# A mixed attention and expert kernel: the second and third expert computed in two row tiles of 64

## The chip, the cores and the metric

The kernel runs on one core of a Trainium2 chip. The engines of a core have a queue each and work side by side: TensorE (matmuls; in the profile PE, its weight loads PEld), VectorE (DVE), ScalarE (ACT), GpSimd (POOL) and SyncE (SP), which here issues DMAs and passes on semaphores. The metric is the device time of one execution in microseconds (us), less being better. Times are the median of several executions; the profile is of one further execution.

## What is computed

The output is `g * a + (1 - g) * b` for 2048 tokens of width 448. `a` is a linear attention with a learned softmax feature map (16 heads of 28), `b` a mixture of 8 experts of which each token uses the best two, `g` a sigmoid gate per token.

```python
def _B_ref(x, w_gate, w1, w2):               # E = 8 experts, K = 2, F = 1792
    logits = xf @ w_gate
    topk_idx = jnp.argsort(-logits, axis=-1)[:, :K]
    topk_val = jnp.take_along_axis(logits, topk_idx, axis=-1)
    gates = _softmax(topk_val, axis=-1)
    for e in range(E):
        mask = (topk_idx == e)
        w = (gates * mask).sum(-1, keepdims=True)
        h = _silu(xf @ w1[e]) @ w2[e]         # 448 -> 1792 -> 448
        out = out + w * h
```

All of it is in float32. The kernel splits each operand of a matmul into a rounded part and a remainder (h and l below) and adds three products: high x high, high x low, low x high.

## The kernel before

**Stages.** The first part computes attention, routing and the table of which token goes to which expert. The expert part follows: one loop (L1321) over `s`, 8 experts times 14 chunks of 128 hidden rows, `e, fc = divmod(s, 14)`. Experts are taken in the order of their number of tokens; `ROOMS` gives the columns kept for each: 552, 544, 544, 504, 504, 504, 496, 488. The first three have more than 512 (`LARGE = 3`); the columns above 512 are their extra ones, `extra(e)`: 40, 32, 32. Where these are 32 the expert is called narrow, and the second layer of the extra columns is done at the end of the expert, for all chunks together, by `side_by_side` from raw weights (L1143), which are kept for it in buffers named `kept`.

**One chunk.** The first layer gives `hp` (128 hidden rows x tokens) in PSUM from the weights w1 and the gathered tokens `xgh`, `xgl`. `gated` puts it through silu on ScalarE (L1076) into `hs`, and VectorE splits that into `hx` (L1082, L1085; the extra columns go to `hxe`, L1080). The second layer multiplies `hx` with w2 and adds into `acc`, one PSUM bank for each 128 tokens (c = 0 to 3, and 4 for the extra ones). After chunk 13 `leave` scales each `acc` into `y` (L1194 on ScalarE for odd c, L1196 on VectorE for even c) and GpSimd scatters it with an indirect DMA that adds into the output (L995).

**Two forms.** Experts 0 to 2 used the full array of 128 rows. `first` (L1054) runs a chunk in two pieces of half the columns (276 or 272), 11 matmuls each (L145): the 448 input rows lie in four groups of 128, the last of them holding 64 rows twice, so that the three products take 4 + 4 + 3 matmuls. `second` and `share` (L1161) run the second layer one or two chunks behind, with the list `held`.

Experts 3 to 7 use two row tiles: the array as two halves of 64 rows that work at the same time, each on its own PSUM bank. `first_pair` (L1046) takes two chunks at once, each with a bank of its own. In `in_halves` (L1031) a round is two matmuls, one in each half. The seven groups of 64 input rows are shared out over 12 rounds and, after a change of sides, 9 turned rounds, in which each bank is written from the other half of the array (L1043). `second_pair` (L1114) does the same for the second layer of two chunks in 24 rounds (L1127). The loop draws these rounds from a generator `queue` with `go_on(n)`, 12 in each chunk: in an even chunk 12 first rounds, 12 second ones, 9 turned ones; in an odd chunk 12 second ones.

**Hand-overs.** The two halves may not write one bank at the same time, and nothing in TensorE's queue orders them. So when a bank goes from one half to the other, `meet` (L1015) puts a nop in SyncE's queue (L1020) which waits for a matmul that lies at most `APART = 24` matmuls back, and the first matmul of the other half waits for the nop. SyncE's queue keeps its order: the nops stand in line with the weight loads of `stage` (L773), and `behind_` ties both into one sequence.

**Order.** TensorE, ScalarE and VectorE have the order written out by the program in the expert part. In each step ScalarE and VectorE first split the weights of a later chunk (`halve`, L796 and L798), and from chunk 9 on transpose and split one tile of the next expert's tokens (`tokens`, L869, L849, L854); from chunk 4 on GpSimd issues two gathers of those tokens per chunk (`gathers`, L829). PSUM has two banks for `hp`, four for `acc` with c = 0, 1 and 4, and one pair for c = 2 and 3.

Of the kernel before, what the change touches and what calls it, by code (L numbers as in the profile page):

```python
# [9 lines left out]
F32R = mybir.dt.float32r  # L10
# [8 lines left out]
P = 128  # L19
# [66 lines left out]
FILL = ((0, 0), (0, 1))  # L86
APART = 24


@with_exitstack  # L90
def gated_mix(ctx: ExitStack, tc: tile.TileContext, xt, xq, wk, wq, wv, wphi, wo, w12, out):
# [765 lines left out]
    def tokens(e, c):  # L857
        if c == 0:
            pool = pf if e % 2 else pw
            xg[e] = (pool.tile([P, 4, CAP], F32R, tag="xgh", name=f"xgh{e}", bufs=1),  # L860
                     pool.tile([P, 4, MAIN] if e >= LARGE else [P, 3, CAP], F32R, tag="xgl", name=f"xgl{e}", bufs=1))
        xgh, xgl = xg[e]
        if (e, c) not in xg:
            return
        t = xg[e, c]
        n, m = (4, P) if c < nm else (-(-extra(e) // 32), extra(e))
        xt_ = pm.tile([P, 4, P], F32, tag="xt", name=f"xgt{e}{c}")
        for b in range(n):
            nc.vector.transpose(xt_[:, :, b * 32:(b + 1) * 32], t[:, b].rearrange("p (c k) -> p c k", c=4))  # L869
        yield  # L870
        m = min(m, ROOMS[e] - c * P)
        at = slice(c * P, c * P + m)
        both(xgh[:, :, at], xgl[:, :, at], xt_[:, :, 0:m], e >= LARGE)

# [155 lines left out]

    def in_halves(o, xh, xl, wh, wl):  # L1031
        rounds = []
        for own, turned_ in (((0, 1, 2, 3), False), ((0, 1, 2), True)):
            for s in own:
                for w, x in ((wh, xh), (wl, xh), (wh, xl)):
                    one = [(1 - a if turned_ else a, a) for a in range(2)]
                    rounds.append([(i, a, w[half[a], s, i * P:(i + 1) * P], x[half[a], s])
                                   for i, a in (reversed(one) if turned_ else one)])
# [7 lines left out]
    def first_pair(e, pair):  # L1046
        n = ROOMS[e]
        xgh, xgl = (x[:, :, 0:n] for x in xg[e])
        hp = [bank("A", f"hp{e}_{2 * pair + i}")[:, 0:n] for i in range(2)]
        yield from in_halves(hp, xgh, xgl, *wts[e * (NFC // 2) + pair, 1])  # L1050
        for i in range(2):
            gated(e, 2 * pair + i, 0, hp[i])

    def first(e, fc, hf):  # L1054
# [37 lines left out]
    def accs(e):  # L1092
        own = [nm, 0, 1] if extra(e) else [0, 1] if e + 1 < E else range(nm)
        a = {c: bank("O", f"acc{e}{c}") for c in own}
# [19 lines left out]
    def second_pair(e, pair):  # L1114
# [3 lines left out]
        if narrow(e) and ends:  # L1118
            for at in range(0, NFC, BATCH):
                side_by_side(e, range(at, min(at + BATCH, NFC)))  # L1120
        todo = [(c, l, r) for c in range(nm) for i in range(2) for l, r in products(e, 2 * pair + i, c)]
        n = len(todo) // 2
# [8 lines left out]
        if ends:  # L1131
            leave(e, (2, 3, *order(e)[:-2]))
            if e == E - 2:
                settle()
# [94 lines left out]
    for t in range(NT + 2):  # L1229
# [67 lines left out]
        if SPLIT <= t < SPLIT + 3 and splits:  # L1297
            if next(splits[0], 0) == 0:
                del splits[0]
                if splits:  # L1300
# [11 lines left out]
    held = []  # L1312
    queue = (h for e, pair in [(LARGE - 1, NFC // 2 - 1), *((e, pair) for e in range(LARGE, E)
                               for pair in range((NFC - LATE * (e == E - 1)) // 2))] for h in second_pair(e, pair))
# [6 lines left out]
    for s in range(E * NFC):  # L1321
        e, fc = divmod(s, NFC)
        k, i = divmod(s, 2)
        token = tokens(e + 1, fc - 9) if e + 1 < E and 9 <= fc <= 9 + nm else iter(())
        next(token, 0)
# [8 lines left out]
        if e + 1 < E and fc >= 4:  # L1334
            for _ in range(2):
                next(asked, None)
        if e < LARGE:
            for hf in range(2):
# [3 lines left out]
            advance(1)  # L1342
            while len(held) > (1 if e == 0 or fc == 0 else 2):
                h = held.pop(0)
# [6 lines left out]
        if e == E - 1 and fc > NFC - LATE:  # L1351
            n = n // 2 if fc < NFC - 1 else 0
        if fc % 2 == 0:
            f = first_pair(e, fc // 2)
# [119 lines left out]
```

## Time and profile before

| what | value |
|---|---|
| median of 3 runs | 792.58 us (791.54 to 792.87) |
| the profiled execution | 790.7 us |
| its span, first to last instruction | 789.0 us |
| mean granted clock of TensorE | 0.995 |
| HBM read, written | 72.31 MB, 12.82 MB |
| instructions | 18466 |

How to read the lines that follow below. In the groups of instructions a row is: line, engine, operation, what it writes <- what it reads, the shape (64*128 is a weight tile of 64 rows and 128 columns), xcount, then busy us and the mean ns of one, then idle us of that engine just before them with what ended it. In the timeline a row starts with the start in us and the length in us; several instructions of one kind are merged. In a row of the waits stands who waited for whom, us in total, times, the longest. Matmuls are pipelined: a matmul's length includes its way through the array, so the price of one in a stream is the distance between two starts.

### The profile page before, as it was taken

Reading aid. Unit: us, or ns where it says so; the run is one execution under the profiler, and the core shown is the slowest. Engines: PE = TensorE matmul, PEld = TensorE weight load, DVE = VectorE, ACT = ScalarE, POOL = GpSimd, SP = SyncE. Lnnn points to the kernel's source line nnn. Section 1 sums busy time; section 2 is a strip of 40 time slices with the busy share of each in tenths; the row PEclk is TensorE's granted clock in tenths of the full one; section 3 lists DMA queues with packets and bytes.
Section 4 is the critical chain, followed back from the end, with each engine's and each line's share of the span. In section 5 each row is a group of like instructions: output and inputs, shape, how many; then the busy total and the mean of one; then the engine's idle time right before and its main releaser. Section 6 shows DMA issues by size and latency. Waiting matters only on the chain. (4 is left out here: it accounts for less than half of the span.)

```text
span 789.0 us, 18466 instructions
## 1 busy us (share of the span) xinstructions
PE 776.7 (98%) x7542; PEld 721.9 (91%) x7542; DVE 481.6 (61%) x1045; ACT 308.9 (39%) x521; POOL 338.3 (43%) x320
## 2 busy tenths in 40 slices
PE   9999999999999999999999998999999999999996
PEld 7888888888999999998998897999999999999995
DVE  4798978778776865665575443544754555475442
ACT  5543455666533443343342322332432333343220
POOL 4667877875123235414540435144325405423102
PEclk9999999999999999999999998999999999999999
DMA  8420000144333336326541452363345436434502
GB/s 282 118 86 1 2 2 26 39 103 143 125 137 127 108 88 179 100 83 144 160 131 54 105 162 90 108 153 128 120 116 152 130 112 157 136 135 116 171 2 47
DMA packets 39756, 86.37 MB, mean 109 GB/s; under 512 B 11338, under 2 KB 20722, under 8 KB 39668
## 3 DMA queue, kind: packets, MB, share of 16 engines
q1 hardware_dynamic: 29332, 67.88, 26.0%
q0 software_dynamic: 10192, 17.03, 11.2%
q8 instruction: 61, 1.00, 0.6%
q10 hardware_dynamic: 144, 0.23, 0.1%
q14 instruction: 27, 0.22, 0.1%
HBM read 72.31 MB, written 12.82 MB: 108 GB/s over the span
## 5 line engine op out<-in xcount | busy, mean ns | idle before, releaser
L829 POOL DMA_INDIRECT xg<-in_xq_dram,idq x114 | 127.1, 1115 | 155.2 <-PE hp L1043 55.5
L1076 ACT ACTIVATE hs<-hp 128x272 f32<-128x272 f32 (+4 forms) x154 | 70.8, 483 | 312.2 <-issue 175.0
L1127 PE MATMUL acc<-w2h,hx 64*128 64x448 f32 (+3 forms) x1088 | 192.0, 363 | 0.1
L1082 DVE CAST hx<-hs 128x504 fp32r<-128x504 f32 (+5 forms) x154 | 55.1, 358 | 209.3 <-ACT hs L1076 196.4
L1127 PEld LDWEIGHTS acc<-w2h,hx 64*128 64x128 f32 (+3 forms) x1088 | 159.8, 182 | 5.0 <-ACT y L1194 1.5
L1127 PE MATMUL acc<-w2l,hx 64*128 64x448 f32 (+3 forms) x544 | 152.4, 364 | 0.0
L1043 PE MATMUL hp<-xgh,w1h 64*128 64x504 f32 (+2 forms) x490 | 144.8, 390 | 2.5 <-issue 2.5
L1043 PE MATMUL hp<-xgh,w1l 64*128 64x504 f32 (+2 forms) x490 | 144.7, 389 | 0.0
L1043 PE MATMUL hp<-xgl,w1h 64*128 64x504 f32 (+2 forms) x490 | 144.4, 388 | 0.0
L995 POOL DMA_INDIRECT out_dram<-y,tabm x30 | 49.3, 1643 | 158.1 <-DVE y L1196 150.8
L1161 PE MATMUL acc<-w2h,hx 128*128 128x448 f32 (+2 forms) x366 | 111.7, 365 | 0.0
L1127 PEld LDWEIGHTS acc<-w2l,hx 64*128 64x128 f32 (+3 forms) x544 | 95.8, 182 | 1.5
L1043 PEld LDWEIGHTS hp<-xgh,w1h 64*128 64x128 f32 x490 | 87.4, 186 | 6.0 <-issue 3.9
L1043 PEld LDWEIGHTS hp<-xgl,w1h 64*128 64x128 f32 x490 | 87.7, 187 | 2.2
L1043 PEld LDWEIGHTS hp<-xgh,w1l 64*128 64x128 f32 x490 | 87.4, 187 | 2.0
L1085 DVE TENSOR_TENSOR hx<-hs,hx 128x276 fp32r<-128x276 f32 (+5 forms) x168 | 84.9, 512 | 5.3
L145 PE MATMUL hp<-xgh,w1h 128*128 128x272 f32 (+1 forms) x336 | 87.9, 289 | 0.0
L145 PE MATMUL hp<-xgh,w1l 128*128 128x272 f32 (+1 forms) x336 | 87.7, 289 | 0.0
L798 DVE TENSOR_TENSOR w1l<-wr,w1h 128x1024 fp32r<-128x1024 f32 x56 | 68.3, 1219 | 11.1 <-ACT w1h L796 9.9
L1161 PEld LDWEIGHTS acc<-w2h,hx 128*128 128x128 f32 (+2 forms) x366 | 68.0, 186 | 6.2 <-issue 0.7
L1161 PE MATMUL acc<-w2l,hx 128*128 128x448 f32 (+2 forms) x190 | 69.4, 365 | 0.0
L145 PEld LDWEIGHTS hp<-xgh,w1h 128*128 128x128 f32 x336 | 63.2, 188 | 0.7
(239 smaller groups left out, 1398.4 us busy)
## 6 DMA issues: line engine op xcount, KB each, us to landing
wr<-in_w_dram SPq DMA_DIRECT2D x56, 512.0 KB
wr<-in_w_dram SPq DMA_DIRECT2D x46, 448.0 KB
kept<-in_w_dram SPq DMA_DIRECT2D x10, 448.0 KB
out_dram<-aos SPq DMA_DIRECT2D x16, 224.0 KB
xr<-in_xt_dram SPq DMA_DIRECT2D x10, 256.0 KB
xg<-in_xq_dram,idq POOLq DMA_INDIRECT x114
xr<-in_xt_dram SPq DMA_DIRECT2D x6, 192.0 KB
out_dram<-zero SPq DMA_DIRECT2D x5, 224.0 KB
```

The costliest lines, as they stand in the source:

```text
L145: reached["pe"] = nc.tensor.matmul(o, a, b, start=i == 0, stop=i == n - 1)
L798: nc.vector.tensor_tensor(out=l, in0=raws[s][layer - 1], in1=h.bitcast(F32), op=ALU.subtract)
L829: i = nc.gpsimd.indirect_dma_start(out=t[:, b], out_offset=None, in_=xq, in_offset=bass.IndirectOffsetOnAxis(ap=idq[:, e, 4 * c + b:4 * c ...
L995: return nc.gpsimd.indirect_dma_start(out=out, out_offset=bass.IndirectOffsetOnAxis(ap=idx_ap, axis=0), in_=y, in_offset=None, compute_op= ...
L1043: meet(("first", i), a, lambda: nc.tensor.matmul(o[i], l, r, start=n == 0, stop=n == len(rounds) - 1), n == 0)
L1076: nc.scalar.activation(hs[:, tsl], hp, AF.Silu)
L1082: nc.vector.tensor_copy(h[:, tsl], hs[:, tsl])
L1085: nc.vector.tensor_tensor(out=h[:, a + o:b + o], in0=hs[:, a:b], in1=h[:, a:b].bitcast(F32), op=ALU.subtract)
L1127: meet((e, c), a, lambda: nc.tensor.matmul(acc[e][c][:l.shape[1], 0:D], l[half[a]], r[half[a]], start=new, stop=ends and c not in of[k + 1 ...
L1161: i = nc.tensor.matmul(acc[e][c][:l.shape[1], 0:D], l, r, start=fc == 0 and k == 0, stop=fc == NFC - 1 and k == len(pr) - 1)
```

## The change

The experts from `TILED = 1` on, so now also 1 and 2, run in row tiles; only expert 0 keeps the full array. For experts 1 and 2, whose 544 columns do not fit in one PSUM bank, a new `first_pieces` gives the two halves of the columns (272) of one chunk to the two banks, with the same 12 and 9 rounds. Their chunk runs 12 first rounds, `LEAD = 6` second rounds, 9 turned rounds and 6 second rounds; the first two chunks of expert 1 run 7 and 7, since they finish the last pair of expert 0, which has 28 rounds. The low part `xgl` of their tokens gets a fourth group.

The banks of `acc` are asked for in another order for experts 1 and 2, their second layer takes c in the order 0, 2, 1, 3, and `LEAVING` gives the order in which the `acc` of experts 0, 1 and 2 are emptied. During expert 0, three gathers are issued per chunk instead of two, and the tokens of expert 1 are split from chunk 8 on. Expert 0 holds its last two chunks back for the queue.

```diff
+LEAVING = ((4, 2, 3, 0, 1), (0, 2, 3, 4, 1), (2, 3, 0, 4, 1))
+TILED = 1
+LEAD = 6
...
-                     pool.tile([P, 4, MAIN] if e >= LARGE else [P, 3, CAP], F32R, tag="xgl", name=f"xgl{e}", bufs=1))
+                     pool.tile([P, 4, MAIN if e >= LARGE else CAP] if e >= TILED else [P, 3, CAP], F32R, tag="xgl", name=f"xgl{e}", bufs=1))
...
-        both(xgh[:, :, at], xgl[:, :, at], xt_[:, :, 0:m], e >= LARGE)
+        both(xgh[:, :, at], xgl[:, :, at], xt_[:, :, 0:m], e >= TILED)
...
-    def in_halves(o, xh, xl, wh, wl):
+    def in_halves(o, ops):
...
-                for w, x in ((wh, xh), (wl, xh), (wh, xl)):
+                for w, x in ((2, 0), (3, 0), (2, 1)):
                     one = [(1 - a if turned_ else a, a) for a in range(2)]
-                    rounds.append([(i, a, w[half[a], s, i * P:(i + 1) * P], x[half[a], s])
+                    rounds.append([(i, a, ops[i][w][half[a], s], ops[i][x][half[a], s])
...
+    def first_pieces(e, fc):
+        s, i = divmod(e * NFC + fc, 2)
+        w = [x[:, :, i * P:(i + 1) * P] for x in wts[s, 1]]
+        n = ROOMS[e] // 2
+        hp = [bank("A", f"hp{e}_{fc}_{hf}")[:, 0:n] for hf in range(2)]
+        yield from in_halves(hp, [(*(x[:, :, hf * n:(hf + 1) * n] for x in xg[e]), *w) for hf in range(2)])
+        for hf in range(2):
+            gated(e, fc, hf, hp[hf])
...
-        own = [nm, 0, 1] if extra(e) else [0, 1] if e + 1 < E else range(nm)
+        own = [nm, 0, 1] if e < TILED else [0, 1, nm] if extra(e) else [0, 1] if e + 1 < E else range(nm)
...
-        todo = [(c, l, r) for c in range(nm) for i in range(2) for l, r in products(e, 2 * pair + i, c)]
+        todo = [(c, l, r) for c in ((0, 2, 1, 3) if narrow(e) else order(e)) for i in range(2)
+                for l, r in products(e, 2 * pair + i, c)]
...
-            leave(e, (2, 3, *order(e)[:-2]))
+            leave(e, LEAVING[e] if extra(e) else (2, 3, 0, 1))
...
-    queue = (h for e, pair in [(LARGE - 1, NFC // 2 - 1), *((e, pair) for e in range(LARGE, E)
+    queue = (h for e, pair in [(TILED - 1, NFC // 2 - 1), *((e, pair) for e in range(TILED, E)
...
-        token = tokens(e + 1, fc - 9) if e + 1 < E and 9 <= fc <= 9 + nm else iter(())
+        at = fc - (9 if e else 8)
+        token = tokens(e + 1, at) if e + 1 < E and 0 <= at <= nm else iter(())
...
-            for _ in range(2):
+            for _ in range(2 if e else 3):
                 next(asked, None)
-        if e < LARGE:
+        if e < TILED:
...
-            while len(held) > (1 if e == 0 or fc == 0 else 2):
+            while len(held) > (1 if fc < NFC - 1 else 2):
...
-        if fc % 2 == 0:
+        if extra(e):
+            a, b = (7, 7) if (e, fc) in ((1, 0), (1, 1)) else (LEAD, n - LEAD)
+            f = first_pieces(e, fc)
+            next(f)
+            go_on(a)
+            next(f, None)
+            go_on(b)
+        elif fc % 2 == 0:
```

More of the change, by code (lines that the diff above doesn't have):

```diff
@@ L1049, in first_pair @@
         hp = [bank("A", f"hp{e}_{2 * pair + i}")[:, 0:n] for i in range(2)]
-        yield from in_halves(hp, xgh, xgl, *wts[e * (NFC // 2) + pair, 1])
+        yield from in_halves(hp, [(xgh, xgl, *(w[:, :, i * P:(i + 1) * P] for w in wts[e * (NFC // 2) + pair, 1]))
+                                  for i in range(2)])
         for i in range(2):
             gated(e, 2 * pair + i, 0, hp[i])
+    def first_pieces(e, fc):
[6 more added lines that the diff above has]
+            gated(e, fc, hf, hp[hf])
     def first(e, fc, hf):
```

## The prediction

> **What bounds the kernel now.** First the page's engine shares, then the timeline of TensorE at one expert of each kind, then the waits.
>
> ```profile
> PE 776.7 (98%) x7542; PEld 721.9 (91%) x7542; DVE 481.6 (61%) x1045; ACT 308.9 (39%) x521; POOL 338.3 (43%) x320
> ```
>
> TensorE (PE) is busy for 776.7 us, 98% of the span, so a change is worth what it takes out of TensorE's own stream, less the waits that it puts in. The chain of waits starts at the very last scatter and says nothing here. The expert stage, with the window rows of one plain chunk, one tiled pair and the one hole:
>
> ```profile
> 340.53:345.72 5.19, 5.19 (x36) 5.02 (x35) 4.28 (x13) 2.38 (x4) 0.94 (x1) 1.00 0.20 36
> 454.45:464.11 9.66, 9.66 (x93) 9.66 (x91) 4.33 (x7) 2.86 (x4) 1.33 (x1) 1.00 0.64 178
> 481.00:484.00 3.00, 0.73 (x4) 0.32 (x3) 0.61 (x2) 1.27 (x3) 2.09 (x3) 0.93 0.82 291
> 484.00:493.00 9.00, 8.78 (x54) 7.97 (x56) 6.40 (x15) 2.85 (x4) 3.94 (x4) 0.64 0.12 31
> ```
>
> Columns: length, then busy time of PE, weight loads (PEld), VectorE (DVE), ScalarE (ACT), GpSimd (POOL), then granted clock, DMA share, GB/s. PE fills the first two windows, at full clock. At 481 us, inside the fourth expert (e=3), it stands for 2.3 and 0.2 us and has a clock of 0.64 for 9 us (a loss of 9 x 0.36 = 3.2): 5.7 us, in a stage whose code the change leaves alone.
>
> A chunk (128 of the 1792 hidden rows) of the second expert (e=1) in the old form, then rounds of the tiled form of e=3:
>
> ```profile
> 337.77 0.29 PE L145 MATMUL hp<-xgh,w1h 128*128 128x272 f32 x1
> ...
> 340.53 0.36 PE L1161 MATMUL acc<-w2h,hx 128*128 128x448 f32 x1
> ...
> 342.96 0.29 PE L145 MATMUL hp<-xgh,w1h 128*128 128x272 f32 x1
> ...
> 439.48 0.37 PE L1127 MATMUL acc<-w2h,hx 64*128 64x448 f32 x2
> ...
> 441.90 0.39 PE L1043 MATMUL hp<-xgh,w1h 64*128 64x504 f32 x2
> ...
> 444.42 0.39 PE L1043 MATMUL hp<-xgl,w1h 64*128 64x504 f32 x2
> ```
>
> First layer: 22 matmuls in 340.53 - 337.77 = 2.76 us, 0.1255 each. Second layer: 12 in 2.43, 0.2025 each. Tiled: 12 rounds of two 64-row matmuls in 441.90 - 439.48 = 2.42, so a round of 448 columns costs what one full matmul of 448 does; a round of 504 costs 2.52 / 11 = 0.229.
>
> **The change part by part.**
>
> *First layer of e=1 and e=2 in row tiles.* The 448 input rows are seven halves of 64, times three products: 21 rounds in place of 22 matmuls, on the same 272 columns. No row shows a tiled round of 272. At the full matmul's price, 0.1255, each chunk saves one: 28 chunks x 0.1255 = **-3.5 us**. Bounds: the line through the tiled 504 (0.229, 0.2286 by the pair: (9.66 - 24 x 0.2025) / 21) and 448 (0.2025) leads to 0.1205 at 272, which would save 21 x 0.005 x 28 = 2.9 us more; from the other side, 0.229 lies 0.002 over the line of the two full rows (0.2025 + 56 x 0.00044 = 0.227), and with more than twice that on top a round would cost 0.131 and save nothing. I take 0.1255: same columns, nearest row.
>
> *Weight loads.* A round has two loads where a full matmul has one.
>
> ```profile
> L730 PE MATMUL et<-ident,eq 64*128 64x64 f32 x224 | 10.0, 229 | 0.0
> L145 PEld LDWEIGHTS hp<-xgh,w1h 128*128 128x128 f32 x336 | 63.2, 188 | 0.7
> ```
>
> The transposes of L730 load 64x128 weights for every matmul, in row tiles: 224 in 10.0 us, 45 ns each, so two loads fit in 89 ns, under 126. Cost nothing. The Trainium skill, "TensorE: Matmul & The Clock Gate", section "LDWEIGHTS (loading the stationary operand)", prices a load by its columns alone, at 1.2 GHz: 128 columns are 107 ns, whatever the rows; two in turn would be 213 ns, a round longer than its matmul. By that rule 21 rounds would be 4.5 us; row L730 speaks against it.
>
> *Second layer.* Rounds and matmuls are equal in number and price: 0. The two readings above, 2.42 and 2.43, tell nothing below a hundredth, and a hundredth in 26 chunks is 0.3; I put in +0.2 (0 to 0.3). The last two chunks of e=0 become a queued pair of 28 rounds for 28 matmuls: 0.
>
> *e=0 into e=1.* The last first-layer piece of (0,13) used to be followed by 14 second-layer matmuls. Now the first rounds of (1,0) come straight behind it and need both hp banks at once. Rows of the release:
>
> ```profile
> 468.54 0.37 PE L1127 MATMUL acc<-w2h,hx 64*128 64x448 f32 x1
> 468.62 0.39 PE L1043 MATMUL hp<-xgl,w1h 64*128 64x504 f32 x1
> ...
> 469.09 1.07 ACT L1076 ACTIVATE hs<-hp 128x504 f32<-128x504 f32 x2 [6.83 <-PE hp L1043]
> ...
> 482.73 1.07 ACT L1076 ACTIVATE hs<-hp 128x504 f32<-128x504 f32 x2 [10.78 <-remote]
> ...
> 483.38 1.27 PE L1043 MATMUL hp<-xgh,w1h 64*128 64x504 f32 x2 [2.27 <-issue]
> ```
>
> ```profile
> L1076 ACT ACTIVATE hs<-hp 128x504 f32<-128x504 f32 x42 | 22.6, 589 | 121.3 <-issue 66.0 <-PE hp L1043 44.6 <-remote 10.8
> L1076 ACT ACTIVATE hs<-hp 128x272 f32<-128x272 f32 x56 | 22.2, 397 | 75.3 <-PE hp L145 44.6 <-issue 30.7
> ```
>
> Silu starts 469.09 - 469.01 = 0.08 after the last matmul's end; PE starts 483.38 - (482.73 + 0.59) = 0.06 after silu's. So from the start of the last matmul: 0.29 + 0.08 + 0.40 + 0.06 = 0.83, where the next would have started after 0.13: **+0.7 us**, once. The hole's 2.3 us cost 3.2 more by the lowered clock; 0.7 us is a third of it, and I let it cost 0.7. The Trainium skill, "TensorE: Matmul & The Clock Gate", section "HAM oscillation — how this bites in real kernels", puts the limit at gaps of some 3.4 us; by it neither gap would lower the clock, and the hole's 2.3 us did.
>
> *Six rounds ahead of the turned ones.* Each chunk now runs 12 first rounds, 6 second, 9 turned first, 6 second. Two things must fit in six rounds (6 x 0.2025 = 1.22 us). One: SyncE sees the last of the 12 and frees the banks for the other row tile: 0.29 + 0.08 to see it, 0.06 to start, 0.19 a load = 0.62, in 1.22 + 0.13 = 1.35: spare 0.7.
>
> ```profile
> L1020 SPq EVENT_SEMAPHORE  x132: 17/17/17, 435.4 to 769.0; - x132
> SPq L773 <- PE acc L1143: 15.9, 1, 15.9
> L1127 PE MATMUL acc<-w2h,hx 64*128 64x448 f32 x824 | 179.4, 363 | 0.1
> ```
>
> 132 hand-overs now leave PE 0.1 us idle on L1127, with 12 rounds of cover. I put in +0.2 us for all new ones (0 to 1). Queued behind a hand-over on SyncE are the weight loads of L773, and the reverse: the load of e=2's third pair waits for the raw weights that L1143 still reads (15.9 us in one wait), and the first hand-over of pair (1,6) stands behind it. L1143 is done with that buffer after its second batch of four:
>
> ```profile
> 358.60 0.96 PE L1143 MATMUL acc<-wr,hxe 128*32 128x448 f32 x8
> 359.37 2.06 PE L1143 MATMUL acc<-kept,hxe 128*32 128x448 f32 x24
> ```
>
> ```profile
> 273.29 0.33 SPq L773 DMA_DIRECT2D kept<-in_w_dram  x1
> ```
>
> That is some 0.7 us into the 2.0, and the load's issue takes 0.33: hidden, 0.5 us once if not. Two: both silus after the turned rounds must free both hp banks before the next chunk. Silus start (1.07 - 0.59) = 0.48 apart at 504, 0.48 - 0.19 = 0.29 at 272: 0.29 + 0.08 + 0.29 + 0.40 + 0.06 = 1.12 of 1.35. Spare 0.2 us, the thinnest cover of the change; cost 0, priced as a rival.
>
> *Orders at expert changes.* At (1,2) and (2,2) the second bank of the new expert is the one that the first y of the old expert leaves; VectorE comes to it after the chunk's hx work.
>
> ```profile
> L1082 DVE CAST hx<-hs 128x272 fp32r<-128x272 f32 x28 | 8.8, 313 | 31.1 <-ACT hs L1076 28.6 <-issue 2.5
> L1082 DVE CAST hx<-hs 128x240 fp32r<-128x240 f32 x28 | 8.3, 296 | 0.0
> L1085 DVE TENSOR_TENSOR hx<-hs,hx 128x272 fp32r<-128x272 f32 x28 | 12.4, 443 | 1.0
> L1085 DVE TENSOR_TENSOR hx<-hs,hx 128x240 fp32r<-128x240 f32 x28 | 11.5, 409 | 1.0
> L1080 DVE COPY hxe<-hs 128x32 f32<-128x32 f32 x28 | 5.5, 196 | 13.1 <-ACT hs L1076 12.5 <-issue 0.6
> L1196 DVE TENSOR_SCALAR y<-acc,tabm 128x448 f32<-128x448 f32 x15 | 9.8, 679 | 2.6 <-PE acc L1161 2.5
> ```
>
> From the last turned matmul: first silu 0.77, five operations 1.66, y 0.68, release 0.06: 3.17 us. PE needs the bank after 0.13 + 1.22 + 12 x 0.1255 = 2.85. Up to 0.3 late each; the rows overlap a little, so 0 to 0.3: **+0.4** for both. The other banks have six rounds more. For e >= 3 the order is unchanged.
>
> *First gather sooner.* 17 indirect DMAs are issued in six chunks of e=0 in place of nine, three per chunk; one takes GpSimd 0.94 us (the only one in the first window above), so 2.8 us of a chunk of over 5, on an engine that is busy 43%. The token work moves from chunks 9 to 13 to chunks 8 to 12, the same VectorE and ScalarE operations plus one larger subtraction for two: off the path. It answers the 14 x 0.2025 = 2.8 us that no longer lie between (0,13) and (1,0). If that cover is gone: the length of a token step's tail, about 1 us once.
>
> **Sum:** -3.5 + 0.2 + 0.7 + 0.2 + 0.4 = -2.0 us, in the profiled execution from 790.7 (span 789.0) to 788.7. The median of the runs is 792.58, 1.9 above the profiled one; I carry the difference over: **790.6 us**. A measurement of this kernel can tell about 0.2%, 1.6 us, from no change: faster is below 791.0, slower above 794.2.
>
> **The rivals.**
>
> *Silu's cover is too short (slower).* The two row tiles do not march in step: in the tiled pair one starts its second layer at 468.54 while the other's last first-layer matmul starts at 468.62, and a tile that is ahead takes from the 0.2 us spare. If the next chunk waits 0.17 us on average in 26 chunks, that is 4.4 us: 795.0. It decides from 2.0 / 26 = 0.08 us per chunk. For it: spare 0.2 only, ScalarE also serves weight splits. Against: a tile that is ahead has slack itself, and ScalarE is busy for 2.38 of 5.19 us in a chunk, with that work lying before the silus.
>
> *The change does not do what it says:* a round of 272 in tiles costs 0.131, 21 are worth 22, and only the 1.5 us of waits remain: 794.1.
>
> *Two loads bind the round.* If loads go no faster than a 504 round proves (0.229 for two), 21 rounds take 4.8 us: +2.05 x 28 = 57 us, 848. L730 all but rules it out. It is the skill's price of a load that points this way.
>
> *The hole at 481 goes* (or is smaller), because the work before it is shifted: another 5.7 us, 785. Nothing in the diff touches what it waits for (ScalarE's silu, put down to "remote"), and it can as well be in no run that is timed.
>
> **How the numbers follow.** Forecast 0.60 (0.42 faster, 0.18 same), silu's cover 0.15 (0.13 slower, 0.02 same), no shorter round 0.11 (0.06 same, 0.05 slower), loads 0.02 slower, the hole 0.12 faster. Faster 0.54, same 0.26, slower 0.20. The range goes down to the cheaper round (790.6 - 2.9 = 787.7, with 0.7 more if no wait comes) and up past the silu case: 787.0 to 795.6; the hole's case and the dear ends above are left out, 0.2 in all.
>
> **What would show it.** In the new trace: starts of L1043 of 272 columns 0.1255 apart per round (right) or 0.13 and more (wrong); a chunk of e=1 in 5.07 us in place of 5.19; idle time of PE before the first L1043 of (1,0) of 0.7 us, released by ScalarE; none before the other chunks of e=1 and e=2 (a regular 0.1 to 0.3 there is the silu rival); no PE wait ended by SyncE. A second hole with a lowered clock anywhere, or the present one missing, would make the time wrong by 3 to 6 us without touching the working above.

## The result, and the profile after

The changed kernel took **799.64 us** (median of 6 runs, 797.94 to 800.46) where the kernel before, beside it, took 792.24 (791.2 to 792.87): a ratio of 1.0102, 95% interval 1.0089 to 1.0116. Forecast were 790.6 us and a range of 787.0 to 795.6. The profiled execution took 799.95 us, with a span of 798.2. From the page of the changed kernel, the busy line, the granted clock in 40 slices, and the group of its first layer with the idle time ahead of it at the end:

```profile
PE 777.8 (97%) x8442; PEld 725.9 (91%) x8442; DVE 475.0 (60%) x1035; ACT 306.3 (38%) x521; POOL 339.4 (43%) x320
PEclk9999999999999999999989998999999999999999
L1046 PE MATMUL hp<-xgh,w1h 64*128 64x272 f32 (+3 forms) x882 | 216.1, 345 | 8.4 <-SPq L1023 4.1
```

Three windows of the same execution (length, then busy time of PE, weight loads, VectorE, ScalarE, GpSimd, then clock, DMA share, GB/s): chunks of e=2, later chunks of e=2, and e=3.

```profile
377.00:387.00 10.00, 10.00 (x136) 9.95 (x134) 5.01 (x12) 3.09 (x6) 3.13 (x3) 1.00 0.61 159
395.00:410.00 15.00, 10.52 (x100) 9.16 (x98) 2.59 (x6) 1.75 (x4) 10.32 (x10) 0.80 0.39 115
485.00:497.00 12.00, 7.73 (x47) 5.59 (x46) 3.40 (x9) 2.35 (x4) 7.59 (x8) 0.83 0.39 126
```

The first window is what was forecast: PE is full. Apart from the chunks at the two expert changes and the places named next, the chunks of e=1 and e=2, read off the starts of their first L1046, are 5.05 to 5.16 us long, against 5.19 before. The loss is local. In 15 us of e=2 PE stands for 4.5 us and then runs at a lower clock (0.50 for some 6.8 us); chunk (2,8) takes 12.5 us. The hole in e=3 is longer than before (a gap of 3.9 us in place of 2.3), and (1,5) loses 1.5 us. Against a stream of matmuls at the prediction's prices the three places cost 8.1, 2.3 more than before, and 1.5; with some 0.8 at the expert changes and -3.4 in the regular chunks that makes +9.3, and the spans differ by 9.2.

The timeline of the worst place, TensorE (PE) and GpSimd (POOL):

```profile
400.16 0.39 PE L1046 MATMUL hp<-xgl,w1h 64*128 64x272 f32 x2
400.42 1.55 POOL L832 DMA_INDIRECT xg<-in_xq_dram,idq  x1 [0.30 <-issue]
401.83 0.47 PE L1141 MATMUL acc<-w2h,hx 64*128 64x448 f32 x2 [1.28 <-SPq L1023]
...
402.92 0.41 PE L1141 MATMUL acc<-w2h,hx 64*128 64x448 f32 x2
403.52 0.94 POOL L832 DMA_INDIRECT xg<-in_xq_dram,idq  x1 [0.30 <-issue]
404.77 0.94 POOL L832 DMA_INDIRECT xg<-in_xq_dram,idq  x1 [0.30 <-issue]
405.44 0.59 PE L1046 MATMUL hp<-xgh,w1h 64*128 64x272 f32 x1 [2.11 <-SPq L1023]
406.02 0.94 POOL L832 DMA_INDIRECT xg<-in_xq_dram,idq  x1 [0.30 <-issue]
406.83 0.59 PE L1046 MATMUL hp<-xgh,w1h 64*128 64x272 f32 x1 [0.81 <-SPq L1023]
```

The last of the first rounds ends at 400.55. The turned rounds need only to know that; SyncE's nop (L1023) waits for nothing else and SyncE issues nothing else in this stretch, and yet they start at 405.44. The nop got TensorE's semaphore 4.8 us late. Meanwhile GpSimd issues gathers without a pause, ten of them from 395.15 to 408.20, one every 1.25 to 1.85 us. The semaphore events of the trace say the same by themselves: when the updates of TensorE's semaphore are set beside the modelled ends of the matmuls that raise it, they are late only where gathers stand close together and nowhere else in the expert stage: about 0.85 us behind a pair in e=1 and e=2, and up to 2.3, 6.2 and 3.5 us in the trains of four and of ten gathers that begin at 306, 395 and 477 us. Not every such place shows it (several runs of four in the later experts stay below 0.1 us), and the scatters alone show none. The waits of the changed kernel (who for whom, us in total, times, longest):

```profile
PEld hp L1046 <- SPq L1023: 5.1, 3, 2.5
PE hp L1046 <- SPq L1023: 4.1, 3, 2.1
PE hp L1046 <- ACT hs L1089: 4.1, 2, 3.9
```

The trains were in the profile of before already. There GpSimd's timeline has, up to the silu of the prediction's hole, this (the last of them spaced alike):

```profile
475.28 0.94 POOL L829 DMA_INDIRECT xg<-in_xq_dram,idq  x1 [0.30 <-issue]
476.53 0.94 POOL L829 DMA_INDIRECT xg<-in_xq_dram,idq  x1 [0.30 <-issue]
...
481.53 0.94 POOL L829 DMA_INDIRECT xg<-in_xq_dram,idq  x1 [0.30 <-issue]
```

The scatters of the extra columns (L998, up to four of them, each waiting for the one before to land) hold GpSimd's queue for 20 us and more behind an expert change; the gathers meant two to a chunk pile up behind them and then go out in a run. One thing is different there. By the same measure the semaphores of the kernel before are at most 0.01 us late behind the pairs of e=1, and 0.8 us in a run of ten gathers beside e=2 (384.7 to 398.0 us), both computed in the full-array form; the 3.2 us behind its hole belong to e=3, which is tiled.

**Theory T1**: trains of gathers make TensorE's semaphores late; the old form of e=1 and e=2 had some 3 us of cover against that, the tiled form 0.1 to 0.7. **Rivals**: T2, the covers are short in every chunk; T3, the gathers' traffic is at work, not their issue; and, from the first results on, T4, the lateness belongs to the chip.

### The profile page after: what moved, and what is told of

It is laid out like the page before. It is cut to its first block, busy times and chain, and to the rows that moved or that the text cites. A ratio compares the mean times of both kernels' runs of the same rounds, so it can differ in the third digit from the quotient of the medians.

```text
span 798.2 us, 20347 instructions
## 1 busy us (share of the span) xinstructions
PE 777.8 (97%) x8442; PEld 725.9 (91%) x8442; DVE 475.0 (60%) x1035; ACT 306.3 (38%) x521; POOL 339.4 (43%) x320
## 5 line engine op out<-in xcount | busy, mean ns | idle before, releaser
L1141 PE MATMUL acc<-w2h,hx 64*128 64x448 f32 (+4 forms) x1540 | 276.1, 364 | 1.7 <-SPq L1023 1.3
L1046 PE MATMUL hp<-xgh,w1h 64*128 64x272 f32 (+3 forms) x882 | 216.1, 345 | 8.4 <-SPq L1023 4.1
L1141 PEld LDWEIGHTS acc<-w2h,hx 64*128 64x128 f32 (+4 forms) x1540 | 215.7, 184 | 7.6 <-ACT y L1208 1.6
L1046 PE MATMUL hp<-xgh,w1l 64*128 64x272 f32 (+3 forms) x882 | 214.7, 344 | 0.0
L1046 PE MATMUL hp<-xgl,w1h 64*128 64x272 f32 (+3 forms) x882 | 214.1, 343 | 0.0
L1141 PE MATMUL acc<-w2l,hx 64*128 64x448 f32 (+4 forms) x772 | 203.2, 364 | 0.1
L1046 PEld LDWEIGHTS hp<-xgh,w1h 64*128 64x128 f32 x882 | 142.1, 187 | 14.3 <-ACT hs L1089 5.6
L1046 PEld LDWEIGHTS hp<-xgl,w1h 64*128 64x128 f32 x882 | 141.7, 187 | 1.9
L1046 PEld LDWEIGHTS hp<-xgh,w1l 64*128 64x128 f32 x882 | 141.6, 187 | 1.8
L1141 PEld LDWEIGHTS acc<-w2l,hx 64*128 64x128 f32 (+4 forms) x772 | 125.5, 184 | 1.2
L998 POOL DMA_INDIRECT out_dram<-y,tabm x30 | 49.2, 1640 | 177.5 <-DVE y L1210 170.4
L799 ACT ACTIVATE w1h<-wr 128x1024 fp32r<-128x1024 f32 x56 | 59.2, 1057 | 0.0
L1175 PE MATMUL acc<-w2h,hx 128*128 128x448 f32 (+2 forms) x140 | 42.9, 366 | 0.0
L998 POOL DMA_INDIRECT out_dram<-y,tabx x10 | 15.3, 1534 | 64.2 <-DVE y L1210 38.8
```

Source lines behind the costliest of these rows:

```text
L799: nc.scalar.activation(h, raws[s][layer - 1], AF.Copy)
L998: return nc.gpsimd.indirect_dma_start(out=out, out_offset=bass.IndirectOffsetOnAxis(ap=idx_ap, axis=0), in_=y, in_offset=None, compute_op= ...
L1046: meet(("first", i), a, lambda: nc.tensor.matmul(o[i], l, r, start=n == 0, stop=n == len(rounds) - 1), n == 0)
L1141: meet((e, c), a, lambda: nc.tensor.matmul(acc[e][c][:l.shape[1], 0:D], l[half[a]], r[half[a]], start=new, stop=ends and c not in of[k + 1 ...
L1175: i = nc.tensor.matmul(acc[e][c][:l.shape[1], 0:D], l, r, start=fc == 0 and k == 0, stop=fc == NFC - 1 and k == len(pr) - 1)
```

## The experiments

Each group ran on one chip, with the kernel before beside it. The number is the chip's; "in time" and "late" are my words for the two sorts that turned up.

| chip | before, us | kernel: median us, ratio to before with its 95% interval |
|---|---|---|
| first measurement | 792.24 | changed: 799.64, 1.0102 (1.0089 to 1.0116) |
| 14, in time | 784.0 | a_defer: 780.95, 0.9953 (0.9937 to 0.9970); b_defer: 783.85, 0.9999 (0.9989 to 1.0008); a_reuse: 781.39, 0.9959 (0.9945 to 0.9973); b_reuse: 784.05, 0.9998 (0.9989 to 1.0008) |
| 2, in time | 784.3 | changed (a_again): 780.77, 0.9957 (0.9940 to 0.9973); a_defer2: 780.76, 0.9957 (0.9943 to 0.9971) |
| 4, in time | 784.65 | a_silu: 791.75 and b_silu: 787.15 (one run each); a_lead8: 788.4, 1.0051 (1.0035 to 1.0068); a_lead2: 781.55, 0.9960 (0.9947 to 0.9972) |
| 3, in time | 784.09 | a_safe: 780.58, 0.9955 (0.9939 to 0.9972); a_late: 780.82, 0.9962 (0.9947 to 0.9976) |
| 0, late | 789.61 | a_wide: 780.72, 0.9885 (0.9849 to 0.9920) |
| 6, late | 791.38 | changed (a_third): 799.72, 1.0120 (1.0087 to 1.0152); a_defer3: 785.95, 0.9925 (0.9903 to 0.9948) |
| 11, late | 790.92 | a_spread: 786.03, 0.9946 (0.9929 to 0.9964); b_defer2: 784.67, 0.9926 (0.9909 to 0.9943) |
| 7, in time | 784.21 | a_calm: 780.19, 0.9948 (0.9932 to 0.9965) |

### The trains taken away, in both kernels

Deferred scatters (a_ from the changed kernel, b_ from the kernel before):

```diff
+                met["gather"] = i
...
+    later = []
+    def one_later():
+        e, v, ids = later.pop(0)
+        i = scatter_add(v, ids)
+        after(i, done[e - 1] if e else rows_done)
+        follow(i, met["gather"])
+        done[e].append(i)
...
+            if c == nm:
+                later.extend((e, v, ids) for v, ids in todo)
+                continue
...
+        if later and fc in (4, 6, 8, 10):
+            one_later()
```

No gathers for experts 2 to 7, which compute on the tokens of expert 1 instead (reuse):

```diff
     def gathers(e):
+        if e > 1:
+            xg.update({(e, c): xg[1, c] for c in range(nm + (extra(e) > 0))})
+            return
```

> The changed kernel, with the scatters of the extra columns not issued in one run behind the four main scatters of an expert but one each in chunks 4, 6, 8 and 10 of the next expert, behind that chunk's gathers. All work is kept. GpSimd's queue is then free when the gathers are asked for, so no train of four and more gathers stands in it. Theory T1 (while GpSimd issues gathers back to back, the others see TensorE's semaphores late, and the tiled form of e=1 and e=2 has only 1.2 us of cover for that): the idle gaps of TensorE at 310 us and 398 to 407 us and the one in e=3 vanish with their lowered clock, some 1.5 + 8.1 + 8.5 us less: 781 to 785 us, and no chunk of e=1 or e=2 but the first two is longer than 5.3 us. Theory T2 (the covers of silu and SyncE are too short in every chunk, whatever GpSimd does): no change, 798 to 801. Theory T3 (the gathers' traffic, not their issue, disturbs the others): the same bytes are moved with more spacing, so 785 to 795, the gaps smaller and spread over more chunks.

> The kernel before the change, with the same deferral of the extra columns' scatters. All work is kept. T1: the hole at 481 us of e=3 is the same thing as the gaps of the changed kernel, so it goes with its lowered clock, 5.5 us: 785.5 to 788 us. T2, by which the hole in e=3 belongs to something else: 792, unchanged. T3: 787 to 791.

> The changed kernel without the gathers of experts 2 to 7: they compute on the tokens of expert 1, so the output is not the reference's; scatters, token work and all matmuls are kept. T1 and T3: no gather after 340 us, so no gap of TensorE after that, and only the one at 310 us (the gathers of e=2 during e=1) gone too: 780 to 785 us. T2: 798 to 801.

> The kernel before the change, again without the gathers of experts 2 to 7 (tokens of expert 1 used in their place; the output is not the reference's). T1 and T3: the hole at 481 us goes, 785 to 788 us. T2: 792, unchanged. Beside a_reuse it gives the price of the change without gathers: by the prediction's sum a_reuse should be about 2 to 3.5 us below b_reuse.

The times of the two a_ kernels look like T1: 781. But b_defer and b_reuse are equal to the unaltered kernel before, which on this chip took 784.0, 8 us less than in the first measurement. There was no hole to take away. And in none of the four traces is a semaphore late behind a pair of gathers, where the first measurement had 0.85 us. The runs settle nothing on T1; T4 comes up. T2 falls: the covers are the same here, and the chunks of a_defer are 5.05 to 5.08 us long.

### The changed kernel on another chip

No edit for a_again; a_defer2 is a_defer once more.

> The changed kernel itself, unaltered. The four kernels before ran on a chip where the kernel before takes 784.0 us and not 792.2, and their traces show no late semaphore of TensorE at all, not even behind pairs of gathers that stood as close as in the first trace. So two readings are open. T1 (trains of gathers on GpSimd delay TensorE's semaphores, on any chip): the changed kernel has its gaps in every place, 10 to 18 us above the version with deferred scatters. T4 (the late semaphores belong to the chip or the moment, not to the program): where the kernel before takes about 784, the changed one takes 780 to 783, with no gap but the 0.2 us at (1,0), and where it takes 792, the changed one takes 798 to 801.

> The version with deferred scatters again, beside the unaltered one on the same chip. T1: 10 to 18 us below the unaltered changed kernel wherever it runs. T4: the same as the unaltered one within 2 us where the kernel before takes 784; where that takes 792, T4 says nothing and T1 says 781 to 785.

T4's number: 780.77, and a_defer2 the same. Here the change makes the kernel 0.43% faster. From the page of a_again:

```profile
PE 769.3 (99%) x8442; PEld 724.7 (93%) x8442; DVE 477.3 (61%) x1035; ACT 305.8 (39%) x521; POOL 338.3 (43%) x320
PEclk9999999999999999999999999999999999999998
L1046 PE MATMUL hp<-xgh,w1h 64*128 64x272 f32 (+3 forms) x882 | 219.9, 340 | 0.2 <-ACT hs L1089 0.2
```

and the windows of the same stages:

```profile
375.00:385.00 10.00, 10.00 (x134) 9.83 (x132) 4.93 (x12) 3.07 (x7) 2.75 (x2) 1.00 0.61 161
395.00:410.00 15.00, 15.00 (x200) 14.99 (x198) 10.35 (x29) 5.87 (x12) 12.21 (x10) 1.00 0.45 151
485.00:497.00 12.00, 12.00 (x116) 11.94 (x114) 8.55 (x18) 5.71 (x10) 6.17 (x6) 1.00 0.36 121
```

From 395 to 410 us GpSimd issues ten gathers here too, a little further apart (busy 12.21 us), and pairs of them elsewhere as close as in the first measurement; PE is full, at full clock, and of 8.4 us idle ahead of L1046 0.2 are left. So a train of gathers alone does not make a semaphore late: it does so on some chips, or at some moments.

### How much cover each form has

To price a late hand-over on a chip that is in time, I made the lateness myself: extra silus, and other values of LEAD.

```diff
+        for _ in range({(1, 4): 3, (1, 8): 6, (2, 8): 12}.get((e, fc), 0) if hf == 0 else 0):
+            nc.scalar.activation(hs[:, tsl], hp, AF.Silu)
         nc.scalar.activation(hs[:, tsl], hp, AF.Silu)
```

```diff
-LEAD = 6
+LEAD = 8
```

> The changed kernel with the first silu of three chunks done several times over: 3 extra ones of 272 columns at (1,4), 6 at (1,8), 12 at (2,8). From the prediction's working two silus of this size start 0.29 us apart, so both silus of these chunks come some 0.9, 1.7 and 3.5 us late. It stands for a late semaphore of one known length, on whatever chip. The prediction gave the silus 0.2 us to spare in the tiled form of e=1 and e=2. If that is the cover, TensorE stands 0.7, 1.5 and 3.3 us behind those chunks, and the last one lowers the clock as the hole of 2.3 us did: 5.5 us of stalls and some 3 us of slow clock, 785 to 791 us where the unaltered changed kernel takes 780.8. If the cover is larger (a theory by which the late semaphores of the first measurement needed no thin cover, only their length), the first two leave no gap.

> The kernel before with the same extra silus in the same three chunks. In its form the next use of a bank comes some 3.8 us after its last matmul (11 matmuls of the other piece and 12 of the second layer), so 3.3 us are to spare: no gap from the first two, 0 to 0.5 us from the third, 784 to 785 us. If the plain form were as sensitive as the tiled one, 789 to 793.

> LEAD = 8: eight second rounds before the turned ones and four after, in every chunk of e=1 and e=2 but the first two. The silus' cover falls by 2 x 0.2025 = 0.41 us, from 0.2 to spare to 0.2 short. If the prediction's working of that cover holds, TensorE waits 0.2 us in each of 26 chunks: 5 us more than the unaltered changed kernel, 786 (784 to 787). If the two tiles that are out of step absorb it, or the silus are earlier than worked out: 781.

> LEAD = 2: two second rounds between the first and the turned rounds, so SyncE's hand-over has 0.13 + 0.41 = 0.54 us in place of 1.35 and needs 0.62 by the prediction's working: 0.1 us short in 26 chunks, 2 us more than the unaltered changed kernel, 783 (782 to 784.5). If SyncE is as quick as TensorE's own turn, 781; if a hand-over is dearer than worked out (the nop stands behind weight loads, or takes 0.3 us more), 788 or more.

An extra silu cost 0.43 us, not 0.29 (12 of them took 5.1 us), so the delays are 1.3, 2.6 and 5.1 us. In a_silu the first two delays cost 1.2 and 2.5 us, over their chunk and the next one together: **the cover is 0.1 us**. The third lengthens its own chunk by 4.8 us and costs 2.7 us more in the next one, at the lowered clock (7.75 us in place of 5.06). Windows around the three in a_silu:

```profile
305.00:311.00 6.00, 5.39 (x67) 4.92 (x65) 2.44 (x6) 2.55 (x7) 3.89 (x4) 1.00 0.41 93
322.00:334.00 12.00, 10.09 (x130) 9.62 (x128) 5.95 (x16) 5.65 (x13) 4.06 (x4) 1.00 0.30 93
398.00:416.00 18.00, 13.54 (x140) 13.15 (x138) 7.15 (x19) 9.04 (x21) 9.79 (x10) 0.81 0.42 136
```

The gaps of 0.6 and 1.9 us leave the clock at 1.00; that of 4.5 lowers it, as in the first measurement. In b_silu one wait is left of all three:

```profile
PE hp L145 <- ACT hs L1078: 1.9, 1, 1.9
```

5.1 us late, 1.9 us of stall: the old form had some 3.2 us of cover, where 3.3 was worked out. a_lead8 is 7.6 us above a_again, 0.29 per chunk: taking 0.41 away from the silus leaves them 0.29 short, so 0.12 was to spare. No wait of PE shows this, since the matmuls of the waiting half are recorded as longer; it is read off the chunks, 5.34 us in place of 5.06. a_lead2 is 0.8 us above a_again, 0.03 per chunk: SyncE's hand-over needs little more than the 0.54 us that it had. These runs were on another chip than a_again; before differs by 0.35 us between the two.

### The sooner gather undone, and more cover

```diff
-        at = fc - (9 if e else 8)
+        at = fc - 9
...
-            for _ in range(2 if e else 3):
+            for _ in range(2):
```

That is a_late; a_safe is a_defer with `LEAD = 4`.

> The changed kernel without the sooner first gather: two gathers per chunk during e=0 and the tokens of e=1 split from chunk 9 on, as before the change. The prediction put this edit at 0 and, with its cover gone, at about 1 us once: 780.8 to 782 where the kernel before takes 784, with a gap of TensorE ahead of (1,0) if the tokens are late.

> Deferred scatters and LEAD = 4: the silus' cover grows by 0.41 us, from 0.1 to 0.5 to spare, and SyncE's shrinks as much, which the run with LEAD = 2 priced at nothing or nearly. If the kernel before takes about 784 here (semaphores in time): as the unaltered changed kernel, 780 to 782, since its chunks of 5.06 us are full already. If it takes about 792 (semaphores late behind gathers): by T1 780 to 785, because there are no trains any more and lone pairs of gathers come 0.85 us late at most; by the theory that on such a chip any gather disturbs, 788 to 796.

Both as on a chip that is in time: 780.82 and 780.58. The sooner gather is worth nothing there, as the prediction had it; a_late has no gap ahead of (1,0) but the 0.17 us of a_again.

### A chip with late semaphores again: issue or traffic

In a_wide one gather of 2 KB rows fetches a tile's tokens in place of four of 512-byte rows; inside a tile the tokens come in another order.

```diff
+            if c < nm and e > 1:
+                i = nc.gpsimd.indirect_dma_start(
+                    out=t.rearrange("p a k -> p (a k)"), out_offset=None, in_=x_rows,
+                    in_offset=bass.IndirectOffsetOnAxis(ap=idm[:, e * nm + c:e * nm + c + 1], axis=0))
+                after(i, [reached["pe"]])
+                for _ in range(4):
+                    yield
+                continue
```

> The changed kernel with one gather of 128 rows of 2 KB in place of four of 512 B for each 128 tokens of experts 2 to 7 (the tokens come in another order inside a tile, so the output is not the reference's): the same bytes, a quarter of GpSimd's issues, no trains. Where the kernel before takes 784 here: 780 to 782, nothing to win. Where it takes 792: T1 (GpSimd's issuing in trains delays the semaphores) 780 to 785; T3 (the traffic of the gathers delays them) 792 to 801, with gaps of TensorE while the gathers run.

On chip 0 the kernel before took 789.61 us. With a quarter of the issues and the same bytes the changed kernel took 780.72, and PE is full through the stage that had the long gaps:

```profile
375.00:410.00 35.00, 35.00 (x462) 34.95 (x460) 20.01 (x52) 12.03 (x24) 9.61 (x8) 1.00 0.50 149
```

The latest semaphore of the expert stage is 0.53 us late, behind a pair of these gathers. GpSimd's DMA queue moved the same bytes, first in a_third (a run of the unaltered changed kernel that follows below), then in a_wide (packets, MB, share of 16 engines):

```profile
q0 software_dynamic: 10192, 17.03, 11.2%
q0 software_dynamic: 9040, 17.03, 11.0%
```

Against T3, for T1. The 1152 packets fewer are 16 for each of the 72 issues left out, so a_wide does not tell the issue from what comes with every issue. The unaltered changed kernel was not run on this chip; the next two were run side by side.

### The trains taken away on a late chip

> The changed kernel, unaltered. The last occasion had the kernel before at 789.6 us, lone semaphores of TensorE up to 0.5 us late in the trace of the kernel with wide gathers, and fewer separate semaphore updates on record (6914 where the occasions at 784 have 8900 and the first measurement 7214). If this run meets that condition again (before at 788 to 793): 796 to 801, with the gaps of the first trace in its places, by T1 and T4 both; if the change is harmed only by an accident of the first measurement, 781 to 790. If it meets the other (before at 784): 780.8 again.

> The changed kernel with deferred scatters, beside it. If the kernel before takes 788 to 793 here: T1 (trains of gathers make the semaphores late, on such an occasion) 781 to 786, with lateness of at most 0.9 us behind pairs of gathers and no gap over 1 us; if it is not the trains but any gather that does it, 790 to 799. If before takes 784: 780.8 again.

a_third repeats the first measurement to a tenth of a microsecond, 799.72 us, with the gaps in the same chunks ((2,8) takes 12.55 us). From its page and its windows:

```profile
L1046 PE MATMUL hp<-xgh,w1h 64*128 64x272 f32 (+3 forms) x882 | 221.3, 345 | 7.2 <-SPq L1023 3.8
```

```profile
395.00:410.00 15.00, 10.49 (x99) 9.14 (x97) 2.58 (x6) 1.89 (x4) 10.32 (x10) 0.84 0.40 115
485.00:497.00 12.00, 8.06 (x49) 5.70 (x47) 2.85 (x9) 1.91 (x3) 7.56 (x9) 0.73 0.39 125
```

a_defer3, on the same chip:

```profile
L1047 PE MATMUL hp<-xgh,w1h 64*128 64x272 f32 (+3 forms) x882 | 213.3, 343 | 1.9 <-ACT hs L1090 1.7
```

```profile
395.00:410.00 15.00, 14.84 (x189) 14.07 (x187) 8.18 (x21) 4.41 (x10) 7.75 (x7) 1.00 0.38 102
485.00:497.00 12.00, 11.79 (x109) 10.80 (x107) 8.86 (x23) 5.19 (x8) 4.38 (x4) 1.00 0.36 110
```

All work is kept and only the order on GpSimd's queue differs: 13.8 us are gone, the clock is whole, and the latest semaphore is 1.2 us late where it was 6.2. **T1 holds on such a chip**, and there the version with deferred scatters beats both unaltered kernels: ratio 0.9925 to before, where the changed kernel has 1.0120. The time was expected at 781 to 786, and 5 us over the chips in time remain. The largest piece, GpSimd, ScalarE and PE in a_defer3:

```profile
308.85 1.85 POOL L999 DMA_INDIRECT out_dram<-y,tabx  x1 [2.16 <-issue]
311.00 1.02 POOL L832 DMA_INDIRECT xg<-in_xq_dram,idq  x1 [0.30 <-issue]
...
312.33 1.16 POOL L832 DMA_INDIRECT xg<-in_xq_dram,idq  x1 [0.31 <-issue]
313.80 1.55 POOL L832 DMA_INDIRECT xg<-in_xq_dram,idq  x1 [0.30 <-issue]
315.65 0.95 POOL L832 DMA_INDIRECT xg<-in_xq_dram,idq  x1 [0.30 <-issue]
...
318.97 0.68 PE L1047 MATMUL hp<-xgh,w1h 64*128 64x272 f32 x2 [1.32 <-ACT hs L1090]
```

A deferred scatter stands in the queue for its turn, four gathers run up behind it, and PE has a gap of 1.3 us: a small train of the same sort.

### The gathers set apart, and the hole of the kernel before

a_spread is a_safe with the two gathers of a chunk issued apart: the second goes between the first and the turned rounds (in the paired form, three over the even chunk and one in the odd).

```diff
+    def one_more(e, fc):
+        if e + 1 < E and fc >= 4:
+            next(asked, None)
...
-            for _ in range(2 if e else 3):
+            for _ in range(1 if e else 3):
...
             go_on(a)
+            one_more(e, fc)
             next(f, None)
```

> Deferred scatters, LEAD = 4, and the two gathers that a chunk of experts 1 to 6 issues together set apart: one at the chunk's start, one between its 12 first and its 9 turned rounds (in the paired form three over the even chunk, one in the odd one). Where the kernel before takes 788 to 793: T1 and the lateness of 0.9 us behind pairs leave 5.2 us over 780.8 in the version with deferred scatters alone; with the pairs apart and 0.4 us more for the silus 781 to 783, lateness under 0.6 us and no gap over 0.3 us behind (1,0). If a single gather does as much harm as a pair: 784 to 787. Where before takes 784: 780.8, nothing to win.

> The kernel before with deferred scatters. Where the unaltered kernel before takes 788 to 793 here: if its hole in e=3 has the same cause as the changed kernel's gaps (T1), it goes and 784 to 787 remain; if it has another cause, 788 to 793 as before. Where before takes 784: 784.

b_defer2 answers what the first b_defer could not: 784.67 beside 790.92. **The hole in e=3 of the kernel before had the same cause.** It also shows what the change itself is worth on a late chip. With the scatters deferred in both kernels, a_spread took 786.03 us beside the 784.67 of b_defer2 (their runs overlap), and a_defer3 has the same ratio to before, 0.9925, as b_defer2, 0.9926, though on another chip: the row tiles earn nothing there. On chip 14, in time, a_defer took 780.95 beside the 783.85 of b_defer. The window of 475 to 490 us, first of the kernel before in the first measurement, then of b_defer2:

```profile
475.00:490.00 15.00, 12.51 (x84) 11.00 (x83) 6.58 (x16) 4.12 (x6) 9.87 (x10) 0.79 0.36 109
```

```profile
475.00:490.00 15.00, 14.81 (x138) 13.90 (x137) 7.78 (x18) 5.56 (x9) 7.85 (x7) 1.00 0.40 120
```

a_spread is a miss: 786.03, no better than a_defer3 and above the 781 to 783 expected. Its lateness behind lone gathers is 0.2 to 0.6 us, below the pairs' 0.85, and its chunks of (1,8) to (1,13) are back at 5.05 to 5.06 us; but it still has the hold-up behind the deferred scatter, at 311 to 324 us, where two chunks lose 2 us, and its latest semaphore, 2.0 us at 473 us, stands in another short run of gathers. Its profiled run is its fastest (784.06); the medians of the two are from different chips. What else stands in its slower runs no trace shows.

### The last hold-up taken away

a_calm is a_spread with the deferred scatters in chunks 9, 11, 12 and 13.

> As the version with the gathers set apart (deferred scatters, LEAD = 4, a chunk's two gathers apart), with the deferred scatters in chunks 9, 11, 12 and 13 of the next expert in place of 4, 6, 8 and 10, so that none of them, waiting for the one before to land, holds up the gathers behind it: in the last trace such a hold-up left short trains at 310 to 322 and 460 to 474 us. Where the kernel before takes 788 to 793: T1 781 to 783.5 (the gaps at 314 and 318 us gone, lateness under 0.7 us everywhere, as behind the single gathers of that trace), and 786 if what remained was not the trains. Where before takes 784: 780.8, as all versions.

It met a chip that is in time and took 780.19 us, where a_again took 780.77: a tie. What it does on a late chip stays open.

## Why the prediction was wrong

By its own steps:

- **First layer, -3.5: right.** A chunk takes 5.05 to 5.08 us in place of 5.19, also in the first measurement's quiet chunks: 21 x 0.1255 + 12 x 0.2025 = 5.07. On a chip in time the stretch from the first layer of e=0 to that of e=3 is 3.2 us shorter in a_again than in b_defer (224.4 and 227.6 us).
- **Weight loads, 0: right.** By the rule of the Trainium skill that was weighed there, "TensorE: Matmul & The Clock Gate", section "LDWEIGHTS (loading the stationary operand)", 21 rounds, with their two loads in turn, were estimated at 4.5 us; they are 5.06 - 2.43 = 2.63. The trace disagrees with two such loads in turn: it has two weight loads in each round of 0.1255 us. (The other sum on loads has a slip: +57 us on the time before, with the 1.5 us of waits, is 851 and not 848. It moves no chance.)
- **The four terms of waits, +1.5: too dear.** On a chip in time chunk (1,0) is 0.56 us over its matmuls (forecast 0.7), (1,2) and (2,2) wait for nothing (forecast 0.4 for both), and the hand-overs and the second layer show nothing; 3.5 - 3.2 leaves 0.3 in all.
- **Silu's spare 0.2, SyncE's 0.7: about right as distances** (0.12 by LEAD = 8; at LEAD = 2 SyncE's hand-over ran with 0.54 us of cover at 0.03 per chunk). As a rival, a silu regularly late, it did not come: the regular chunks are full.
- **The step that failed** is the pricing of these covers, "cost 0" for the silus and "+0.2 us for all new ones (0 to 1)" for the hand-overs. Both took it that a semaphore of TensorE is seen 0.08 us after the matmul. The silu's row in the prediction's own fence, waiting 10.78 us at 482.73, is one that was released at least 1.5 us late: PE had stood since 481.1, and the prediction set it aside as a hole "in a stage whose code the change leaves alone" of which "nothing in the diff touches what it waits for". What it waits for is TensorE's semaphore behind a train of gathers, and the diff makes two more experts, with two more trains, live on covers of 0.1 to 0.7 us where they had 3.2. On such a chip 1.5 + 8.1 us are lost in e=1 and e=2, and 2.3 more in e=3, whose covers the change leaves alone; why its hole grew no run shows.
- The sentence that "a second hole with a lowered clock anywhere" would make the time wrong by 3 to 6 us named the failure, but it stood outside the range, as an accident without a chance of its own. With the hole's 5.7 us put at each new train it would have been a rival at 796 to 802.
- **The hole goes, 785**: on a chip in time it is gone from the kernel before too, so it gives no gain there, 784.

On a chip in time the prediction's mechanism decides alone: 0.9957 (0.9940 to 0.9973) on chip 2, where 790.6 to 792.58 was 0.9975, a gain of 3.5 us for the 2.0 forecast, since most of the waits did not come. On the late ones the late semaphores decide, 1.0102 and 1.0120. Shown is that, on a late chip, taking the trains away takes the gaps away, in both kernels, and that the chip or the moment matters: the same program, the same trains, no late semaphore elsewhere. Not shown is why chips differ. Each was met once, so a chip and a moment can't be told apart here. Nor is it shown how much of the loss is the cover's and how much the form's: beside e=2 a run of ten gathers made semaphores 0.8 us late in the full-array form and 6.2 us in the tiled one. The old form never needed its 3.2 us there, and no run gives the tiled form a cover of that length.

## What to carry to other kernels

A cover is worth its length against the latest semaphore that the profile shows, not against the usual one: look for the longest wait that nothing explains, see what the other queues did just then, and ask what the new code would do with that same lateness. A run of small indirect DMAs behind a held-up queue is such a place; spreading its cause (here four scatters) cost nothing on a chip in time (780.76 us beside 780.77) and took the changed kernel on a late one from 1.2% above the kernel before to 0.75% below it. The kernel before gains as much by it there, so a remedy is to be tried on both kernels before the change is credited with it. And a change that thins covers is to be timed on more than one chip.

## What the runs showed of the hardware

- On four occasions (the first measurement, chips 0, 6 and 11) semaphore updates of TensorE came late near gathers: 0.2 to 0.9 us behind one or two gathers of 512-byte rows, 0.6 to 6.2 us within longer runs where they were late at all, 0.53 us behind two of 2 KB rows. On five chips (2, 3, 4, 7, 14) they were never more than 0.17 us late in the expert stage. The traces differ in one more thing: of the kernels that issue all these gathers, the late ones hold 7119 to 7401 separate semaphore updates, those in time 8785 to 8988. Updates seem to be merged there; that is a reading, not an experiment.
- Gaps of 1.3 and 1.9 us of TensorE left the granted clock at 1.00 (a_defer3, a_silu). Around a gap of 4.5, and around runs of gaps with one of 2.1 to 3.9 among them, its mean was 0.73 to 0.84 over windows of 12 to 18 us. Inside such a window it is 0.50 for some 6.8 us and 1.00 on both sides; the prediction's 0.64 over 9 us is such a mean. Windows of the kernel before, then of a_third:

```profile
483.60:490.40 6.80, 6.58 (x29) 5.51 (x30) 6.73 (x16) 3.25 (x5) 4.08 (x4) 0.50 0.14 38
488.00:490.50 2.50, 1.63 (x12) 0.79 (x8) 0.00 (x0) 0.00 (x0) 1.89 (x2) 1.00 0.66 190
490.70:497.40 6.70, 3.73 (x16) 2.56 (x17) 3.25 (x9) 2.21 (x4) 3.68 (x4) 0.50 0.35 122
```

- The length of the longest gap does not tell when the clock falls. In a_third it falls at some 490.6 us, ahead of the gap of 3.0 us that begins at 491.1, after 2.5 us in which PE is busy for 1.63 with gaps of 0.2 to 0.4 us. The Trainium skill, "TensorE: Matmul & The Clock Gate", section "HAM oscillation — how this bites in real kernels", puts the limit at gaps of some 3.4 us; the trace of before, where a single gap of 2.3 us was followed by half the clock, disagrees.
